# Attention and two feed-forward layers: the second layer's first product by Strassen's seven half-size products

## The chip, the cores and the metric

The kernel runs on one core of a Trainium2 chip. The metric is device time in microseconds (us) of one execution; of three runs of the kernel before, the median was 1325.76 us (1323.91 to 1326.36).

## The reference

Attention with four sink keys and a window of 128 over 4 batches of 8 heads, 768 positions, head size 64, gives x of 3072 tokens by 512. Two feed-forward layers follow, each with weights of its own (512 by 2048 and 2048 by 512):

```
x = softmax(keep(q @ k.T / 8)) @ v          # 3072 x 512, float32
h = x @ w1_in;  x = (h - tanh(h)) @ w1_out  # layer 1
h = maximum(x @ w2_in, 0);  out = (h * h) @ w2_out   # layer 2
```

All is float32.

## The kernel before

**Arithmetic.** A float32 operand is split into a high part (rounded to the format that TensorE multiplies in one pass) and a low part, the rest; `split` (L138) makes the high part on ScalarE and the low part on VectorE or GpSimd. A product is then three matmuls: high by high, high by low, low by high. The weights come as pairs of 32-bit words; `convert` (L124) makes float32 of them, with one ScalarE instruction and three VectorE instructions (L130 to L132) on integers, and splits the result.

**Tiling.** Both layers work on tiles of T = 384 tokens, NT = 8 of them. The hidden size 2048 is FC = 16 chunks of 128. For each tile j and chunk fc, `mm1` (L441) computes the chunk of h in one PSUM bank: 4 pieces of the 512 inputs, three matmuls each, the weights stationary and 384 tokens moving. `act` (L445) applies the nonlinearity (L452 and L453 in layer 1, L455 and L456 in layer 2) and splits it into gs. `mm2` adds the chunk to the output's accumulators in PSUM, in layer 1 with 12 matmuls of 384 tokens (L473), in layer 2 with 9 of 512 columns (L475). `mm2` of a chunk comes one chunk behind `mm1`, or two (`lag`) in the last tile of layer 1 and in layer 2, where `mm1` takes four PSUM banks in turn. Behind a tile's last chunk, ScalarE and VectorE copy the accumulators to two buffers o (L484, L482), and a DMA writes them to c.x2 in DRAM (L486) or to the output (L488).

**Stages.** Attention of tile 0 comes first. Then, during tile j of layer 1, attention of tile j + 1 runs between the matmuls (`Heads.tick`: score L257 to L261, its reduction on VectorE L262, exponential L269, normalization L279, transposes L309 and L322, product with v L346 to L364). In tile 0, `hook` also converts layer 1's weights. `hook` loads layer 2's weights from the last tile of layer 1 on, into the slots that layer 1's weights leave, and converts one chunk (of both matrices) every 1.4 chunks, through that tile and the first of layer 2. There `fetch` also loads and splits x of layer 2.

**Order.** TensorE runs in the order in which the program is written. The other engines and the DMA queue on SP get theirs from a planner, by priority and its own estimate of when things are ready; on the chip each engine then takes its instructions strictly in that order. `issue_after` keeps a block's instructions behind a named one on its engine.

Of the kernel before, what the change touches and what calls it, by code (L numbers as in the profile page):

```python
# [11 lines left out]
F32 = mybir.dt.float32  # L12
# [7 lines left out]
P = 128  # L20
# [13 lines left out]

FULL = 2 * H
OFF = 11
LEAD = 3
TMP = 8

# [81 lines left out]
    return c.wp.tile([P, 2, DM], dtype, tag=f"{tag}{i}", name=f"{tag}{i}", bufs=1)  # L121


def convert(c, raw, dst):  # L124

    nc = c.nc
    lo, hi = raw[:, :, 0], raw[:, :, 1]
    w = c.sb.tile([P, DM], I32, tag="w_bit", name="w_bit", bufs=3)
    nc.scalar.activation(hi.bitcast(F32), hi.bitcast(F32), AF.Copy, scale=2.0 ** -112)
    nc.vector.tensor_scalar(w, hi, 3, None, ALU.logical_shift_left)  # L130
    nc.vector.scalar_tensor_tensor(w, lo, 29, w, ALU.logical_shift_right, ALU.bitwise_or)  # L131
    nc.vector.scalar_tensor_tensor(w, hi, -2147483648, w, ALU.bitwise_and, ALU.bitwise_or)  # L132
    dst = dst()
    split(c, dst, w.bitcast(F32), nc.gpsimd)
    return dst


def split(c, dst, src, lo_eng):  # L138

    nc = c.nc  # L140
    nc.scalar.activation(dst[:, 0, :], src, AF.Copy)  # L141
    lo_eng.tensor_tensor(dst[:, 1, :], src, dst[:, 0, :].bitcast(F32), ALU.subtract)  # L142
# [22 lines left out]
class Heads:  # L165
# [200 lines left out]
    def gather(self, n):  # L366

        c, nc, s = self.c, self.c.nc, self.st[n]
        h = self.coords(n)[3]
        if h % 2 == 0:  # L370
            self.xf = c.sb.tile([P, T], F32, tag="xf", name="xf", bufs=2)
        dst = self.xf[D * (h % 2) : D * (h % 2) + D, :]
        if n < FULL:
            nc.scalar.activation(dst, s.av[:D, :T], AF.Copy)
            return
        t = c.sb.tile([D, T], F32, tag="t_av", name="t_av", bufs=2)
        nc.scalar.activation(t, s.av[D:, :T], AF.Copy)
        nc.vector.tensor_tensor(dst, s.av[:D, :T], t, ALU.add)

# [44 lines left out]

def ffn(c, layers, xs, hook=None):

    nc = c.nc
    accs = {}

# [15 lines left out]
    def act(l, h, j, fc):  # L445
        t = c.fp.tile([P, T], F32, tag="t", name="t", bufs=2)
        if lag(l, j) > 1 and fc % 2:
            gs = c.sb.tile([P, 3 * WN], F32R, tag="p", name="p", bufs=2)[:, : 2 * T].rearrange("p (a t) -> p a t", t=T)
        else:
            gs = c.fp.tile([P, 2, T], F32R, tag="gs", name="gs", bufs=2)  # L450
        if l == 0:
            c.last_a = nc.scalar.activation(t, h[:, :T], AF.Tanh)  # L452
            c.last_d = nc.vector.tensor_tensor(t, h[:, :T], t, ALU.subtract)  # L453
        else:
            c.last_a = nc.scalar.activation(t, h[:, :T], AF.Relu)  # L455
            c.last_d = nc.vector.scalar_tensor_tensor(t, h[:, :T], 0.0, t, ALU.max, ALU.mult)  # L456
        split(c, gs, t, nc.vector if l > 0 or j > 0 else nc.gpsimd)
        return gs

    def mm2(l, j, fc, gs, q):  # L460
        w = layers[l].get(1, fc)
        if fc == 0 and q == 0:
            accs[l, j] = [c.ps.tile([P, 512], F32, tag="acc", name="acc", bufs=4) for _ in range(KC if l == 0 else T // P)]
        acc = accs[l, j]
        pas = ((0, 0), (0, 1), (1, 0))
        n = len(acc)
        work = [(m, i) for m in range(n) for i in range(3)]
        hw = (len(work) + 1) // 2
        for m, i in work[q * hw : (q + 1) * hw]:
            a, b = pas[i]  # L470
            st = dict(start=(fc == 0 and i == 0), stop=(fc == FC - 1 and i == 2))
            if l == 0:
                nc.tensor.matmul(acc[m][:, :T], w[:, a, ts(m, P)], gs[:, b, :], **st)  # L473
            else:
                nc.tensor.matmul(acc[m], gs[:, b, ts(m, P)], w[:, a, :], **st)  # L475
        if fc == FC - 1 and q == 1:
            for m in range(n):
                o = c.fp.tile([P, 512], F32, tag="o", name="o", bufs=2)
                wd = T if l == 0 else 512
                with c.tc.high_priority(offset=200):  # L480
                    if m % 2:
                        nc.vector.tensor_copy(o[:, :wd], acc[m][:, :wd])  # L482
                    else:
                        nc.scalar.activation(o[:, :wd], acc[m][:, :wd], AF.Copy)  # L484
                if l == 0:
                    nc.sync.dma_start(c.x2[j, m], o[:, :T])  # L486
                else:
                    nc.sync.dma_start(c.out[j * T + m * P : j * T + (m + 1) * P, :], o)  # L488

    pend = []  # L490
    for l in range(2):
# [22 lines left out]
    for p in pend:  # L514
        mm2(*p, 0)
        mm2(*p, 1)


def fetch(c, src):

    x = []
    for kc in range(KC):
        f = c.sb.tile([P, T], F32, tag="xf", name="xf", bufs=2)
        c.nc.sync.dma_start(f, src(kc))
        t = c.xp.tile([P, 2, T], F32R, tag="x", name="x", bufs=8)
# [12 lines left out]


def banded(c):  # L540

    nc, tc = c.nc, c.tc
    with ExitStack() as es:
        pools(c, es)
        layers = [Weights(c, c.w1_in, c.w1_out), Weights(c, c.w2_in, c.w2_out)]
        heads = Heads(c, None)
        x2 = {}
        loaded = 0

        def next_chunk():  # L550
# [23 lines left out]
        done = 0  # L574

        def hook(l, j, fc, q):
            nonlocal done
            if l == 0:
                if j == 0 and q % 2 == 0:
                    next_chunk()  # L580
                f = fc + LEAD - (q == 1)
                if j == 0 and q % 2 == 1 and LEAD <= f < FC:
                    with tc.issue_after(c.last_a.ins), tc.issue_after(c.last_d.ins):
                        layers[0].convert(int(q == 1), f)
                if j + 1 < NT:
                    heads.tick(64 * (j + 1) + OFF + 4 * fc + q)
            tt = (l * NT + j - NT + 1) * FC + fc
            if q == 2 and 2 <= tt < FC + 2:
                for i in range(2):
                    layers[1].load(i, tt - 2)  # L590
            if q == 3:
                while done < FC and 5 + 1.4 * done <= tt:
                    with tc.issue_after(c.last_a.ins), tc.issue_after(c.last_d.ins):
                        for i in range(2):
                            layers[1].convert(i, done)
                    done += 1
            jn = l * NT + j + 1
            if jn >= NT and jn < 2 * NT and fc == 8 and q == 3:
                x2[jn - NT] = fetch(c, lambda kc: c.x2[jn - NT, kc])

        xs = lambda l, j: heads.x[j] if l == 0 else x2[j]
        with tc.manual_schedule(engines={mybir.EngineType.PE}):
            ffn(c, layers, xs, hook)


def general(c):
# [50 lines left out]
    with ExitStack() as es:  # L657
# [3 lines left out]
        def xs(l, j):  # L661
# [8 lines left out]
            return fetch(c, lambda kc: c.x2[j, kc])  # L670

        ffn(c, layers, xs)


@with_exitstack
def kernel(ctx: ExitStack, tc: tile.TileContext, a0, a1, vs, scal,
# [57 lines left out]
```

## Time and profile before

| what | us |
|---|---|
| median of three runs | 1325.76 |
| profiled execution | 1324.8 |
| its span, first to last instruction | 1323.0 |
| TensorE busy | 1271.1 |
| VectorE busy | 692.7 |
| ScalarE busy | 641.1 |
| GpSimd busy | 322.5 |

PE is TensorE's matmuls, PEld its weight loads, DVE VectorE, ACT ScalarE, POOL GpSimd, SP the engine that issues the DMAs. Matmuls overlap each other, so a matmul's own duration is longer than the time from its start to the next one's start. "Idle before" is the time in which an engine had nothing to do before an instruction, and what ended it.

### The profile page before, as it was taken

What the parts mean: (1) busy time and instruction counts of PE and PEld (TensorE: products, weight loads), DVE (VectorE), ACT (ScalarE), POOL (GpSimd) and SP (SyncE); (2) the same over time, 40 slices, a digit from 0 to 9 for tenths busy, and PEclk for the clock granted to TensorE, in tenths of its full rate; (3) what the DMA queues carried; (4) which work ended last, traced back from release to release, by engine and by line L of the source; (5) the groups of instructions that cost most, each with busy time, mean ns of one, the idle gap of its engine ahead of it and who ended that gap; (6) DMA issues with size and microseconds to landing.
All of it is one profiled execution on the core that took longest, in us unless ns stands there. A gap on an engine that the chain in (4) does not pass through costs nothing.

```text
span 1323.0 us, 19096 instructions
## 1 busy us (share of the span) xinstructions
PE 1271.1 (96%) x7152; PEld 1195.9 (90%) x7152; DVE 692.7 (52%) x1568; ACT 641.1 (48%) x1588; POOL 322.5 (24%) x299
## 2 busy tenths in 40 slices
PE   8888899999999999999998988999999999999997
PEld 5777799999999999999998977899999999999996
DVE  7788655666656665556654999322222222222222
ACT  7765665666656666666653555323232323232221
POOL 1555633333323333333321454201010101010000
PEclk9999999999999999999999999999999999999999
DMA  9641221211211212112007830101010101010000
GB/s 366 230 172 43 80 71 58 80 56 48 72 54 58 81 48 69 54 57 81 20 21 233 247 116 1 48 1 48 0 48 1 49 1 48 1 37 1 25 0 27
DMA packets 31814, 91.01 MB, mean 69 GB/s; under 512 B 3664, under 2 KB 11856, under 8 KB 31712
## 3 DMA queue, kind: packets, MB, share of 16 engines
q1 hardware_dynamic: 31712, 89.70, 20.4%
q8 instruction: 58, 0.95, 0.3%
q14 instruction: 44, 0.36, 0.1%
HBM read 77.11 MB, written 12.58 MB: 68 GB/s over the span
## 4 chain that ended last, share of the span: by engine, by line
PE 44%; DVE 3%; issue 3%; DMA 1%; ACT 1%; POOL 0%; SPq 0%; ACTq 0%; DVEq 0%; POOLq 0%
PE acc L475 19%; PE ps_h L441 6%; PE ps_v L441 5%; PE ps_s L441 5%; PE ps_t L441 5%; PE acc L473 2%; DVE w_bit L132 1%; DMA x<-o 1%; DVE w_bit L131 1%; DVE w_bit L130 0%; DMA xf<-x 0%; DVE t L453 0%; DVE p L142 0%; ACT o L484 0%; POOL x L142 0%
## 5 line engine op out<-in xcount | busy, mean ns | idle before, releaser
L441 PE MATMUL ps_h<-x,wi 128*128 128x384 f32 x1776 | 364.3, 343 | 0.8 <-DVE t L453 0.8
L441 PEld LDWEIGHTS ps_h<-x,wi 128*128 128x128 f32 x1776 | 305.8, 189 | 4.8 <-DVE t L453 1.8
L473 PE MATMUL acc<-gs,wo 128*128 128x384 f32 x1440 | 298.9, 344 | 10.4 <-ACT o L484 9.3
L473 PEld LDWEIGHTS acc<-gs,wo 128*128 128x128 f32 x1440 | 246.9, 189 | 14.9 <-ACT o L484 11.1
L142 POOL TENSOR_TENSOR x<-xf,x 128x384 fp32r<-128x384 f32 x64 | 66.8, 1051 | 411.9 <-ACT x L141 409.4
L475 PE MATMUL acc<-wo,gs 128*128 128x512 f32 x576 | 146.2, 397 | 4.2 <-DVE gs L142 2.0
L475 PE MATMUL acc<-wo,p 128*128 128x512 f32 x576 | 143.4, 393 | 1.1 <-DVE p L142 0.9
L141 ACT ACTIVATE gs<-t 128x384 fp32r<-128x384 f32 x184 | 96.3, 524 | 78.0 <-DVE t L456 38.1
L475 PEld LDWEIGHTS acc<-wo,gs 128*128 128x128 f32 x576 | 107.7, 189 | 25.9 <-DVE gs L142 2.7
L209 POOL TENSOR_TENSOR k_l<-qkv,k_h 128x416 fp32r<-128x416 f32 (+1 forms) x48 | 59.5, 1241 | 291.2 <-ACT k_h L208 291.1
L475 PEld LDWEIGHTS acc<-wo,p 128*128 128x128 f32 x576 | 107.1, 188 | 20.9 <-DVE p L142 1.4
L142 DVE TENSOR_TENSOR gs<-t,gs 128x384 fp32r<-128x384 f32 x168 | 97.3, 579 | 41.8 <-ACT gs L141 41.8
L262 DVE CUSTOM_DVE_ANT_0 p<-ps_s,m 128x272 f32<-128x272 f32 (+1 forms) x168 | 70.0, 416 | 87.7 <-PE ps_s L261 86.3
L453 DVE TENSOR_TENSOR t<-ps_h,t 128x384 f32<-128x384 f32 x116 | 64.6, 557 | 88.4 <-ACT t L452 88.4
L269 ACT ACTIVATE p<-p,nm 128x272 f32<-128x272 f32 (+1 forms) x168 | 83.3, 496 | 1.1 <-DVE nm L262 1.1
L441 PE MATMUL ps_v<-x,wi 128*128 128x384 f32 x432 | 82.4, 339 | 0.0
L441 PE MATMUL ps_t<-x,wi 128*128 128x384 f32 x432 | 82.2, 338 | 0.0
L441 PE MATMUL ps_s<-x,wi 128*128 128x384 f32 x432 | 81.7, 337 | 0.0
L441 PEld LDWEIGHTS ps_v<-x,wi 128*128 128x128 f32 x432 | 77.7, 190 | 2.8
L441 PEld LDWEIGHTS ps_t<-x,wi 128*128 128x128 f32 x432 | 77.5, 190 | 2.7
L279 DVE TENSOR_SCALAR p<-p,sm 128x272 f32<-128x272 f32 (+1 forms) x168 | 78.4, 490 | 2.3
L441 PEld LDWEIGHTS ps_s<-x,wi 128*128 128x128 f32 x432 | 77.0, 189 | 2.8
(130 smaller groups left out, 1771.9 us busy)
## 6 DMA issues: line engine op xcount, KB each, us to landing
qkv<-in_a_dram SPq DMA_DIRECT2D x32, 608.0 KB, 3.9
wi<-in_w_in_dram SPq DMA_DIRECT2D x32, 512.0 KB, 4.9
wo<-in_w_out_dram SPq DMA_DIRECT2D x32, 512.0 KB, 4.7
qkv<-in_a_dram SPq DMA_DIRECT2D x24, 504.0 KB, 3.5
x<-o SPq DMA_DIRECT2D x32, 192.0 KB, 3.4
xf<-x SPq DMA_DIRECT2D x32, 192.0 KB, 2.4
out_dram<-o SPq DMA_DIRECT2D x24, 256.0 KB, 2.0
wi<-in_a_dram SPq DMA_DIRECT2D x8, 504.0 KB, 7.5
```

The lines of the kernel that those rows point to most:

```text
L131: nc.vector.scalar_tensor_tensor(w, lo, 29, w, ALU.logical_shift_right, ALU.bitwise_or)
L132: nc.vector.scalar_tensor_tensor(w, hi, -2147483648, w, ALU.bitwise_and, ALU.bitwise_or)
L141: nc.scalar.activation(dst[:, 0, :], src, AF.Copy)
L142: lo_eng.tensor_tensor(dst[:, 1, :], src, dst[:, 0, :].bitcast(F32), ALU.subtract)
L209: nc.gpsimd.tensor_tensor(s.kl[:, :nk], s.k[:, :nk], s.kh[:, :nk].bitcast(F32), ALU.subtract)
L262: nc.vector.tensor_tensor_reduce(out=s.p[:, u, :w], in0=sc[:, :w], in1=self.masks[kind], op0=ALU.add, op1=ALU.min, scale=-SCALE / 2 if ful ...
L269: self.mark[n] = nc.scalar.activation(s.p[:, u, :w], s.p[:, u, :w], AF.Exp, bias=s.nm[:, u : u + 1], scale=-1.0, accum_out=s.sm[:, u : u + 1])
L279: nc.vector.tensor_scalar(s.p[:, u, :w], s.p[:, u, :w], s.sm[:, u : u + 1], None, ALU.mult)
L441: nc.tensor.matmul(h[:, :T], w[:, a, kc, :], x[kc][:, b, :], start=(kc == 0 and i == 0), stop=(kc == KC - 1 and i == 2))
L453: c.last_d = nc.vector.tensor_tensor(t, h[:, :T], t, ALU.subtract)
L473: nc.tensor.matmul(acc[m][:, :T], w[:, a, ts(m, P)], gs[:, b, :], **st)
L475: nc.tensor.matmul(acc[m], gs[:, b, ts(m, P)], w[:, a, :], **st)
```

## The change

The 2048 hidden columns of layer 2 are paired into NG = 8 groups of two chunks, the 512 inputs into two halves, and the tokens into tiles of 512, of two halves of 256. The first product of a group is then a 2 by 2 block product, done with seven block products (Strassen's scheme in Winograd's form) in place of eight. Each is two input pieces by three matmuls of 256 tokens. `first` does four of them, each in its own bank, `rest` three, which are added to banks in use; between and behind them stand the two halves of the second product of the group before. The sums of products are formed by VectorE from PSUM. The sums of weight blocks are formed by `split_in` in the last tile of layer 1, as layer 1's slots come free, and then stay in SBUF; the sums of x by GpSimd (`sum_x`), once for each tile of 512. The scheme's operands are split into high and low parts behind the sums.

Layer 2's weights are converted during tiles 1 to 6 of layer 1 (`early_step`, once a chunk, in half chunks) and written to DRAM: w_in as float32 (c.wi2), w_out already split (c.wo2). `fetch_out` reads w_out for every group again, into four slots. The pool sb of attention is closed at the start of layer 1's last tile, and a pool l2 takes its place; two buffers in sb become one.

```diff
-def convert(c, raw, dst):
+def to_single(c, raw, w):
...
+def convert(c, raw, dst):
+    w = c.sb.tile([P, DM], I32, tag="w_bit", name="w_bit", bufs=3)[:, : raw.shape[1]]
+    to_single(c, raw, w)
     dst = dst()
-    split(c, dst, w.bitcast(F32), nc.gpsimd)
+    split(c, dst, w.bitcast(F32), c.nc.gpsimd)
...
-            self.xf = c.sb.tile([P, T], F32, tag="xf", name="xf", bufs=2)
+            self.xf = c.sb.tile([P, T], F32, tag="xf", name="xf", bufs=1)
...
+    def early_step(self, step):
+        c = self.c
+        with c.tc.issue_after(c.last_a.ins), c.tc.issue_after(c.last_d.ins):
+            if step < 2 * FC:
+                if step == 0:
+                    self.load(c.w2_in, 0)
+                self.convert_in(step)
+                if step + 1 < 2 * FC:
+                    self.load(c.w2_in, step + 1)
+            elif step % 2 == 0:
+                self.load(c.w2_out, step // 2 - FC)
+            else:
+                self.convert_out(step // 2 - FC)
+
+    def fetch_out(self, fc):
+        c, k = self.c, fc % 4
+        if k < 2:
+            t = slot(c, ("wi", "wo")[k], FC - 1, F32R)
+        else:
+            t = c.l2.tile([P, 2, DM], F32R, tag=f"wos{k}", name=f"wos{k}", bufs=1)
+        c.nc.sync.dma_start(t.bitcast(F32), c.wo2[fc])
+        self.wo[fc] = t
...
+    def split_in(self, g):
...
+        for out, x, y in ((t1[:, 0], b2[:, 0], b1[:, 0]), (t1[:, 1], b2[:, 1], t1[:, 0]),
+                          (t2[:, 0], b2[:, 1], b2[:, 0]), (t2[:, 1], b1[:, 1], t1[:, 1])):
+            nc.vector.tensor_tensor(out, x, y, ALU.subtract)
...
+            nc.scalar.activation(d[:, :, 0, :], src, AF.Copy)
+            nc.vector.tensor_tensor(d[:, :, 1, :], src, d[:, :, 0, :].bitcast(F32), ALU.subtract)
...
+    def before(self, fc):
+        for g in range(NG):
+            if fc == (NP * g + 6) // 4 + 2:
+                self.split_in(g)
+                if g + 2 < NG:
+                    self.load_in(g + 2)
+        if fc == FC - 1:
+            for f in range(2):
+                self.fetch_out(f)
...
+    def product(self, j, g, name, bank, start):
+        w, x = self.w[g, name], self.x[j, name]
+        for kc in range(2):
+            for i, (a, b) in enumerate(((0, 0), (0, 1), (1, 0))):
+                self.c.nc.tensor.matmul(bank, w[:, a, kc, :], x[:, b, kc, :], start=start and kc == 0 and i == 0,
+                                        stop=kc == 1 and i == 2, skip_group_check=True)
+
+    def first(self, j, g):
...
+        for name, bank in zip(ORDER, s.ps):
+            self.product(j, g, name, bank, True)
+        nc.scalar.activation(s.u[:, 0, :], s.ps[0], AF.Copy)
+        nc.vector.tensor_tensor(s.u[:, 1, :], s.ps[1], s.u[:, 0, :], ALU.add)
+        nc.vector.tensor_tensor(s.u[:, 2, :], s.ps[2], s.u[:, 1, :], ALU.add)
+        nc.vector.tensor_tensor(s.c[:, 0, :], s.ps[3], s.u[:, 2, :], ALU.add)
...
+    def rest(self, j, g, s):
+        nc = self.c.nc
+        for name, i in zip(ORDER[4:], (0, 2, 3)):
+            self.product(j, g, name, s.ps[i], False)
...
+    def second(self, j, g, s, q):
...
+        seen = ((1, 1), (0, 0)), ((1, 0), (0, 1))
+        for th, f in seen[q]:
+            w, gs = self.wo[2 * g + f], s.g[th, f]
+            for m in range(2):
+                for i, (a, b) in enumerate(((0, 0), (0, 1), (1, 0))):
+                    nc.tensor.matmul(self.acc[2 * th + m], gs[:, b, ts(m, P)], w[:, a, :],
+                                     start=(g == 0 and q == 0 and i == 0), stop=(g == NG - 1 and q == 1 and i == 2))
...
         def hook(l, j, fc, q):
...
+            if 1 <= j < NT - 1 and q == 3:
+                second.early_step((j - 1) * FC + fc)
+            if j == NT - 1:
+                if fc == 0 and q == 0:
+                    c.sb_es.close()
+                    second.open()
+                if q == 3:
                     with tc.issue_after(c.last_a.ins), tc.issue_after(c.last_d.ins):
+                        second.before(fc)
...
-            ffn(c, layers, xs, hook)
+            second.run(ffn(c, layers, lambda l, j: heads.x[j], hook))
```

`open` loads x of the first 512 tokens (1 MB) and w_in of two groups (1 MB), and sums and splits x. `run` goes through the 48 groups in the order first, half of the second product of the group before, rest, the other half; with the first group stand layer 1's last two `mm2`.

## Rows read from the trace of the kernel before

**Rows 1.** The page's first part: busy us, share, count of each engine.
```profile
PE 1271.1 (96%) x7152; PEld 1195.9 (90%) x7152; DVE 692.7 (52%) x1568; ACT 641.1 (48%) x1588; POOL 322.5 (24%) x299
```
**Rows 2.** Busy time by stretches: from:to and length, busy (instructions), clock, DMA.
```profile
95.00:170.30 75.30, 65.03 (x366) 59.70 (x365) 52.89 (x108) 48.64 (x124) 46.17 (x38) 0.98 0.19 62
...
255.70:345.60 89.90, 88.56 (x573) 88.16 (x572) 55.63 (x147) 56.68 (x153) 29.48 (x30) 1.00 0.19 59
...
696.60:777.00 80.40, 73.32 (x400) 72.05 (x399) 61.34 (x83) 36.29 (x72) 27.80 (x21) 0.96 0.69 215
777.00:849.60 72.60, 67.23 (x321) 58.33 (x320) 57.48 (x83) 35.07 (x70) 26.95 (x21) 0.98 0.12 39
849.60:1310.60 461.00, 461.00 (x2316) 418.19 (x2315) 127.43 (x228) 130.02 (x255) 20.06 (x20) 1.00 0.06 20
```
**Rows 3.** Order of time on ACT: start, us, instruction; layer 2's first and seventh tile ends.
```profile
850.18 0.60 ACT L484 ACTIVATE o<-acc 128x512 f32<-128x512 f32 x1
...
1251.62 0.60 ACT L484 ACTIVATE o<-acc 128x512 f32<-128x512 f32 x1
```
**Rows 4.** Order of time on PE in layer 2.
```profile
1261.15 2.27 PE L441 MATMUL ps_h<-x,wi 128*128 128x384 f32 x12
1263.26 2.24 PE L475 MATMUL acc<-wo,gs 128*128 128x512 f32 x9
1265.34 1.92 PE L441 MATMUL ps_s<-x,wi 128*128 128x384 f32 x10
```
**Rows 5.** Order of time on PE beside attention, matmuls of 256 columns.
```profile
311.50 0.28 PE L350 MATMUL ps_v<-pt,v_s 128*128 128x256 f32 x1
311.61 0.28 PE L353 MATMUL ps_v<-pt,v_s 128*128 128x256 f32 x1
311.73 0.22 PE L350 MATMUL ps_v<-pt,v_s 128*128 128x128 f32 x1
```
**Rows 6.** Groups by line on DVE: count, busy us, mean ns, idle before.
```profile
L131 DVE SCALAR_TENSOR_TENSOR w_bit<-wi,w_bit 128x512 int32<-128x512 int32 x32 | 32.7, 1023 | 0.4
...
L132 DVE SCALAR_TENSOR_TENSOR w_bit<-wi,w_bit 128x512 int32<-128x512 int32 x32 | 25.8, 805 | 0.0
...
L130 DVE TENSOR_SCALAR w_bit<-wi 128x512 int32<-128x512 int32 x32 | 14.6, 457 | 1.6 <-issue 0.7 <-ACT wi L129 0.4
...
L296 DVE TENSOR_TENSOR pt<-ps_t,pt 128x256 fp32r<-128x256 f32 x24 | 10.0, 417 | 0.3 <-ACT pt L294 0.3
```
**Rows 7.** DMA issues: count, KB each, median us from issue to landing.
```profile
wo<-in_w_out_dram SPq DMA_DIRECT2D x32, 512.0 KB, 4.7
```
**Rows 8.** Order of time on DVE and PE in tile 0.
```profile
101.41 0.69 DVE L131 SCALAR_TENSOR_TENSOR w_bit<-wo,w_bit 128x512 int32<-128x512 int32 x1
102.14 1.63 DVE L132 SCALAR_TENSOR_TENSOR w_bit<-wo,w_bit 128x512 int32<-128x512 int32 x1
...
104.19 1.27 PE L257 MATMUL ps_s<-qkv 128*128 128x272 f32 x2 [2.80 <-DVE nm L262]
```
**Rows 9.** Waits: who waited for whom, us in total, times, longest.
```profile
PE acc L473 <- ACT o L484: 9.3, 7, 3.4
```
**Rows 10.** Order of time at the start of layer 1's last tile.
```profile
703.52 0.49 ACT L484 ACTIVATE o<-acc 128x384 f32<-128x384 f32 x1 [5.03 <-DMA x<-o]
...
704.07 2.02 PE L473 MATMUL acc<-gs,wo 128*128 128x384 f32 x6 [3.38 <-ACT o L484]
...
705.89 3.13 PE L441 MATMUL ps_v<-x,wi 128*128 128x384 f32 x12
...
708.86 2.24 PE L473 MATMUL acc<-p,wo 128*128 128x384 f32 x12
```
**Rows 11.** Order of time near the end of layer 1's last tile.
```profile
771.71 3.10 PE L473 MATMUL acc<-p,wo 128*128 128x384 f32 x11 [2.31 <-DVE p L142]
```
**Rows 12.** Order of time at the turn to layer 2, evictions.
```profile
777.00 0.48 ACT L484 ACTIVATE o<-acc 128x384 f32<-128x384 f32 x1
...
780.82 0.49 ACT L484 ACTIVATE o<-acc 128x384 f32<-128x384 f32 x1 [1.68 <-DMA x<-o]
```

More of the change, by code (lines that the diff above doesn't have):

```diff
@@ L36 @@
 OFF = 11
+T2 = 512
+HT = T2 // 2
+NG = FC // 2
+NP = 7
 LEAD = 3
@@ L375, in gather @@
             return
-        t = c.sb.tile([D, T], F32, tag="t_av", name="t_av", bufs=2)
+        t = c.sb.tile([D, T], F32, tag="t_av", name="t_av", bufs=1)
         nc.scalar.activation(t, s.av[D:, :T], AF.Copy)
@@ L447, in act @@
         if lag(l, j) > 1 and fc % 2:
-            gs = c.sb.tile([P, 3 * WN], F32R, tag="p", name="p", bufs=2)[:, : 2 * T].rearrange("p (a t) -> p a t", t=T)
+            gs = c.spare(fc)[:, : 2 * T].rearrange("p (a t) -> p a t", t=T)
         else:
@@ L485, in mm2 @@
                 if l == 0:
-                    nc.sync.dma_start(c.x2[j, m], o[:, :T])
+                    nc.sync.dma_start(c.x2[m, :, ts(j, T)], o[:, :T])
                 else:
@@ L490, in ffn @@
     pend = []
-    for l in range(2):
+    for l in range(len(layers)):
         for j in range(NT):
@@ L513, in ffn @@
                 pend.append((l, j, fc, gs))
-    for p in pend:
-        mm2(*p, 0)
-        mm2(*p, 1)
+    return [lambda p=p, q=q: mm2(*p, q) for p in pend for q in range(2)]
 def fetch(c, src):
@@ L522, in fetch @@
     for kc in range(KC):
-        f = c.sb.tile([P, T], F32, tag="xf", name="xf", bufs=2)
+        f = c.sb.tile([P, T], F32, tag="xf", name="xf", bufs=1)
         c.nc.sync.dma_start(f, src(kc))
@@ L544, in banded @@
         pools(c, es)
-        layers = [Weights(c, c.w1_in, c.w1_out), Weights(c, c.w2_in, c.w2_out)]
+        layers = [Weights(c, c.w1_in, c.w1_out)]
         heads = Heads(c, None)
-        x2 = {}
+        second = Second(c)
         loaded = 0
@@ L573, in banded @@
                     layers[0].convert(i, fc)
-        done = 0
         def hook(l, j, fc, q):
[L577 to L582, printed above, removed]
-                    with tc.issue_after(c.last_a.ins), tc.issue_after(c.last_d.ins):
[L584 to L601, printed above, removed]
+            if j == 0 and q % 2 == 0:
+                next_chunk()
+            f = fc + LEAD - (q == 1)
+            if j == 0 and q % 2 == 1 and LEAD <= f < FC:
+                with tc.issue_after(c.last_a.ins), tc.issue_after(c.last_d.ins):
+                    layers[0].convert(int(q == 1), f)
+            if j + 1 < NT:
+                heads.tick(64 * (j + 1) + OFF + 4 * fc + q)
+            if 1 <= j < NT - 1 and q == 3:
[5 more added lines that the diff above has]
+                if q == 3:
+                    with tc.issue_after(c.last_a.ins), tc.issue_after(c.last_d.ins):
+                        second.before(fc)
         with tc.manual_schedule(engines={mybir.EngineType.PE}):
-            ffn(c, layers, xs, hook)
+            second.run(ffn(c, layers, lambda l, j: heads.x[j], hook))
 def general(c):
@@ L669, in xs @@
                 return fetch(c, lambda kc: c.x1[b * H + 2 * kc : b * H + 2 * kc + 2, :, half * T : (half + 1) * T].rearrange("h d s -> (h d) s"))
-            return fetch(c, lambda kc: c.x2[j, kc])
-        ffn(c, layers, xs)
+            return fetch(c, lambda kc: c.x2[kc, :, ts(j, T)])
+        for m in ffn(c, layers, xs):
+            m()
 @with_exitstack
@@ L684 @@
     c.x1 = dram.tile([B * H, D, S], F32, tag="x1", name="x1")
-    c.x2 = dram.tile([NT, KC, P, T], F32, tag="x2", name="x2")
+    c.x2 = dram.tile([KC, P, B * S], F32, tag="x2", name="x2")
+    c.wi2 = dram.tile([FC, P, DM], F32, tag="wi2", name="wi2")
+    c.wo2 = dram.tile([FC, P, 2, DM], F32, tag="wo2", name="wo2")
     scalars(c)
```

143 lines of the change are left out of this document (141 added, 2 removed).

## The prediction

> **What bounds the kernel now.** I read the first part of the page, then busy time by stretches cut at the tiles of 384 tokens, then TensorE's order of time. In the page [rows 1] the reader is to see that TensorE is busy for 96% and nobody else for more than 52%. The stretches [rows 2] say where the other 4% lies. From 255.7 to 345.6 us (one tile of layer 1 beside attention) TensorE is busy for 88.56 of 89.90 us; from 849.6 to 1310.6 us (layer 2 behind its first tile) for all of 461.00. So there the number of matmuls and the time of one decide. Between lie 696.6 to 849.6, the last tile of layer 1 and the first of layer 2, where time is lost while layer 2's weights are converted. A tile of layer 2 undisturbed takes (1251.62 - 850.18) / 6 = 66.91 us [rows 3]; the first one took 72.6, so 5.7 is lost. A tile of layer 1 without attention is 16 times 24 matmuls of 384 columns; 12 of these take 2.11 us from start to start [rows 4], so 67.5 us. The last one took 80.4: 12.9 lost. Together 18.6.
>
> **The first product (removed and added).** Now, each pair of weight chunks and 384 tokens takes 24 matmuls of 384 columns, 4.22 us; 8 tiles by 8 pairs make 64 x 4.22 = 270.1 us. Changed, each pair and 512 tokens takes seven products of six matmuls of 256 columns: 42, and 6 x 8 x 42 = 2016. A 256-column matmul appears with attention: two of them start at 311.50 and end their turn at 311.73 [rows 5], 0.115 us each. By the slope of the long ones (2.11 / 12 = 0.176 at 384 columns, 2.08 / 9 = 0.231 at 512) [rows 4] it would be 0.121. I take 0.118, between them, because the rows with 256 columns are only two in a row and rounded: 2016 x 0.118 = 237.9 us. **Saving 32.2 us**, with bounds of 26.2 (0.121) and 38.3 (0.115). The second product keeps 1152 matmuls of 512 columns, hence its time.
>
> The rest of the new layer must hide behind 42 x 0.118 + 24 x 0.231 = 10.5 us of TensorE for each group. VectorE has ten instructions in it, nine of 256 elements and one of 512: at 0.417 us for a 256-element one from PSUM [rows 6] and twice that for the long one, 4.6 us. ScalarE has six short ones. GpSimd has one subtraction a group and eleven longer ones a tile of 512; at its mean of 322.5 / 299 = 1.08 us [rows 1], (48 + 66) x 1.08 = 123 us in 504. In order of time: between the last of a group's seven products and its reuse of a bank stand at least 12 matmuls of 512 columns (2.77 us), and the squares are wanted a whole group later. TensorE fills in with the second product of the group before. So cost nothing; were this cover gone (a PSUM sum on the path, 0.417 us, in each of 48 groups) it would be 20 us. Reloading w_out: 1 MB a group, each of its two DMAs 4.7 us to landing [rows 7], asked for a group ahead: hidden by 10.5 us.
>
> **The weights' conversion (moved).** From the last tile of layer 1 and the first of layer 2 it goes into tiles 1 to 6 of layer 1, as 64 half chunks. A whole chunk takes VectorE 0.457 + 1.023 + 0.805 = 2.29 us [rows 6], a half about 1.2 with its fixed part. 64 x 1.2 = 77 us more VectorE. These tiles now have it busy for 55.63 of 89.90 us (62%) [rows 2]; tiles 1 and 2 get 16 halves each and rise to some 83%, tiles 3 to 6 get 8 each (some 72%). Average room is not the question: VectorE and the other queues are in order, and behind a conversion stand the score's reduction (L262), which frees the score's PSUM bank, the subtraction after tanh (L453), which frees the only bank of the first product, and attention's low parts. That is what tile 0 shows: L132 of a conversion from 102.14, then TensorE's score matmul at 104.19, 2.80 us late [rows 8]. The price of it there: 65.03 of 75.30 us busy [rows 2], 10.3 us lost with 26 whole chunks, or 0.2 us for a half. By this 64 halves cost 12.8 us. A gain is excluded, since TensorE has under 1.4 us idle in such a tile, at its end. I take half, **6 us**: a half chunk is three short instructions where tile 0 has two chunks in a row beside GpSimd's subtractions, and attention there runs in full precision mode. The steps' own DMAs (a load of 256 KB, a store of 128 or 256 KB) stand in SP's queue, each behind the conversion it waits for, ahead of q, k, v loads two heads early (cover: a head's 10 us) and of layer 1's stores. The latter matter: at tile ends TensorE waits for the output buffers already, 9.3 us in 7 times [rows 9]. I add **1 us**, bounds 0 and 6 (1 us in each of six ends).
>
> In the same rows L132 lasts 1.63 us and its mean is 0.805, so GpSimd beside it shows. The Trainium skill (SBUF — State Buffer, on the port pair that VectorE and GpSimd share) says that the one that starts first holds the pair for its whole instruction and the other fully blocks. The trace agrees with the long L132. Without it, an L131 takes 0.69 us [rows 8] where its mean is 1.023; if both logical instructions took that, a half would be 0.92 us and the 77 us would be 59, and the term of 6 would shrink towards 4.6.
>
> **The last tile of layer 1 and the turn.** Today's loss of 18.6 us goes, and three things are late next.
> (a) At its start the stores of the tile before compete with loads. Now ScalarE's eviction waits 5.03 us for its buffer, TensorE 3.38 us, and the 18 matmuls behind it run at about half speed (704.07 to 708.86 is 4.79 us, where 18 x 0.176 = 3.17) [rows 10]: 5.0 us. The change puts 2 MB of x and weights in the same place, where now 512 KB chunks come; I keep **5**, bounds 0 and 10.
> (b) Eight times, two chunks are combined (four VectorE subtractions of 256, then three of 512 and one of 256): about 5 x 0.417 + 3 x 0.83 = 4.6 us, 37 us in the tile, with 16 x 1.1 for its own: 55 of 67.5 us. Now the conversion's VectorE fills 61.34 of 80.40 [rows 2] and costs 12.9 - 5.0 = 7.9; TensorE waits 2.31 us at 771.71 for a low part [rows 11]. Less work without GpSimd beside it: I take **1**, bounds 0 and 7.9.
> (c) At the turn, the second product's first group needs the last accumulators and w_out's slot 15. The third eviction now starts 3.82 us after the first (777.00 to 780.82) [rows 12] for want of a buffer; the load of the slot starts only behind the last matmul of layer 1 and lasts 4.7 us [rows 7], while TensorE has 24 x 0.118 = 2.8 us of new products to do. That is 2 us late, and 1 for what the three stores beside it take: **3**, bounds 0 and 7.
> So 18.6 turns into 9: **9.6 us gained**, bounds 18.6 and, with all three at their worst, 6 lost.
>
> **Others.** Five ends of 512-token tiles have four evictions instead of three with two buffers: 1 us in all, bounds 0 and 5; the tail's fourth eviction 0.3.
>
> **Sum.** -32.2 - 9.6 + 6 + 1 + 1.3 = -33.5 us. The profiled execution took 1324.8 us (span 1323.0 and 1.8 around it): 1291.3. The median of the runs is 1.0 above it: 1292.3, put at 1292.
>
> **The rivals.**
> R1, all clean: the combining, the turn and the conversions hide wholly and (a) goes. For it: tiles 1 to 6 lose only at their ends today. Against: 2 MB of loads in (a). 1292 - 6 - 9 = 1277.
> R2, losses stay: the last tile and the turn cost today's 18.6, the conversions tile 0's price of 12.8. 1292 + 9.6 + 6.8 = 1308. For it [rows 8]; against, less VectorE work in both places.
> R3, slower: the conversions become the bound of tiles 1 to 6, at VectorE's queue ahead of the score's reduction. Tile 0's wait of 2.80 us comes with two whole chunks, four halves: 0.7 us a half, 64 x 0.7 = 45 us instead of 6: 1331. It decides from 0.6 us a half on (39.5 / 64). Against: of 26 chunks in tile 0 a few alone paid that.
> R4, slower: weight loads bind. Every matmul loads 128 columns, and the changed layer has 3168 of them instead of 2688. In layer 2 loads are busy for 418.19 us in 2315 [rows 2], 0.181 each; 3168 x 0.181 = 573 us instead of 504: 1292 + 69 = 1361. Against: two matmuls with a load each within 0.23 us [rows 5], so loads overlap. The Trainium skill (Perfetto Trace Analysis, Identifying the Most-Contended Engine) takes the busy share of LDWEIGHTS for TensorE's roofline, not that of matmuls; by that rule layer 2 at 91% has no room for 18% more loads, and R4 would hold. The trace bears it out little.
>
> **Chances.** Forecast 0.62 (1284 to 1301), R1 0.14, R2 0.14, R3 0.07, R4 0.03. Faster by over 0.2% (about what a measurement of this kernel tells from none): forecast, R1, R2, less the edge of R2: 0.88. Within 0.2%: 0.03, from between R2 and R3. Slower: 0.09. The range reaches from R1 to a little beyond R2: 1277 to 1312.
>
> **What would show it.** The product line has 2016 matmuls of 256 columns, starting 0.118 us apart; TensorE 100% busy in layer 2, with 63 us for six groups. Tiles 1 to 6 are 1 us longer on average, with waits for L262, L453 or L279. TensorE's waits for evictions stay at the last tile's start, and one of about 3 us stands at the turn. Wrong would be: matmuls 0.125 us or more apart, tiles 1 to 6 longer by over 3 us each, or TensorE under 97% in layer 2.

## The result and the profile after

The changed kernel takes 1303.9 us (median of 4, 1303.17 to 1305.74) against 1326.06 us beside it: 0.9837 of the time, 95% interval 0.982 to 0.9855. Forecast was 1292, the range 1277 to 1312. The profiled execution took 1303.22 us, its span 1301.3, 21.7 us less than before.

The page's first part, after [rows 1]:

```profile
PE 1245.7 (96%) x7632; PEld 1167.3 (90%) x7632; DVE 816.4 (63%) x2004; ACT 644.6 (50%) x1690; POOL 396.5 (30%) x381
```

TensorE is still busy for 96%. VectorE has 124 us more. Where this lies is told by the stretches, cut where a tile's first accumulator is evicted (from:to and length, busy us of PE, PEld, DVE, ACT, POOL with instructions, clock, DMA) [rows 2]:

```profile
170.80:260.80 90.00, 88.51 (x547) 84.93 (x546) 68.13 (x197) 59.78 (x166) 28.66 (x30) 1.00 0.44 131
260.80:360.70 99.90, 91.76 (x567) 86.99 (x567) 74.55 (x193) 62.35 (x167) 29.96 (x29) 1.00 0.39 117
...
716.40:787.00 70.60, 67.71 (x404) 67.39 (x403) 51.22 (x103) 36.91 (x76) 16.96 (x13) 1.00 0.32 100
787.00:875.00 88.00, 85.51 (x529) 77.35 (x528) 45.16 (x93) 22.90 (x58) 25.40 (x23) 0.98 0.37 117
875.00:1291.50 416.50, 416.13 (x2599) 376.27 (x2598) 206.81 (x442) 111.17 (x274) 83.68 (x79) 1.00 0.38 119
```

The second of these is tile 2 of layer 1: 99.9 us where it was 89.9. The last is layer 2 behind its first tile, with TensorE busy all the time. Layer 2's order of time on PE (start, us, instruction) [rows 4]:

```profile
1001.14 2.91 PE L747 MATMUL acc<-wos,x 128*128 128x512 f32 x12
1003.89 0.88 PE L696 MATMUL ps_h<-xop,wi 128*128 128x256 f32 x6
1004.60 0.88 PE L696 MATMUL ps_s<-xop,wo 128*128 128x256 f32 x6
1005.32 0.88 PE L696 MATMUL ps_t<-xop,wi 128*128 128x256 f32 x6
1006.04 0.88 PE L696 MATMUL ps_v<-xop,wo 128*128 128x256 f32 x6
1006.76 1.55 PE L747 MATMUL acc<-wo,x 128*128 128x512 f32 x6
```

Four products take 2.87 us, so a matmul of 256 columns starts every 0.120 us; the second product's 12 take 2.75.

Put together by stretches, in us of the spans:

| stretch | before | after | difference | forecast |
|---|---|---|---|---|
| up to tile 0's end | 169.8 | 170.8 | +1.0 | 0 |
| tiles 1 and 2 | 175.8 | 189.9 | +14.1 | } +7 |
| tiles 3 to 6 | 351.0 | 355.7 | +4.6 | } |
| last tile of layer 1, 67.5 clean | 80.4 | 70.6 | -9.8 | } -9.6 |
| first tile of layer 2, above a clean one | 6.3 | 3.8 | -2.5 | } |
| layer 2's tiles, clean (8 x 66.91, 6 x 84.16) | 535.3 | 505.0 | -30.3 | -32.2 |
| other ends of layer 2 | 4.5 | 5.5 | +1.1 | +1.3 |

(A tile is measured from its predecessor's first eviction to its own, hence 6.3 where the prediction's stretch gave 5.7.) The differences were taken before rounding and sum to -21.7. One term is far off: the conversions in tiles 1 to 6 cost 18.7 us, not 7.

What TensorE and ScalarE wait for in tile 2 (who waited for whom: us, times, longest):

```profile
ACT wos L132 <- DMA wos<-in_w_in_dram: 15.9, 16, 2.3
ACT p L278 <- DVE nm L271: 12.9, 11, 2.0
...
PEld ps_s L269 <- DVE nm L271: 7.6, 7, 2.2
```

The first row is new: in each of the tile's 16 chunks ScalarE stands until the raw weights have landed. One such place in order of time:

```profile
295.87 0.37 SPq L574 DMA_DIRECT2D wos<-in_w_in_dram  x1
...
298.66 0.45 ACT L132 ACTIVATE wos<-wos 128x256 f32<-128x256 f32 x1 [0.96 <-DMA wos<-in_w_in_dram]
...
299.01 0.51 ACT L150 ACTIVATE gs<-t 128x384 fp32r<-128x384 f32 x1
...
299.54 0.49 ACT L386 ACTIVATE t_av<-ps_v 64x384 f32<-64x384 f32 x1
...
300.72 0.30 DVE L133 TENSOR_SCALAR w_bit<-wos 128x256 int32<-128x256 int32 x1
...
301.66 1.11 DVE L135 SCALAR_TENSOR_TENSOR w_bit<-wos,w_bit 128x256 int32<-128x256 int32 x1
302.69 0.43 DVE L271 CUSTOM_DVE_ANT_0 p<-ps_s,m 128x272 f32<-128x272 f32 x1
...
303.18 0.39 PE L269 MATMUL ps_s<-k_h,q_s 128*128 128x272 f32 x1 [1.30 <-DVE nm L271]
303.21 0.38 SPq L574 DMA_DIRECT2D wos<-in_w_in_dram  x1
```

The load is issued at 295.87 and used at 298.66, and meanwhile tanh's high part (L150) and attention's eviction (L386) stand behind it on ScalarE. VectorE's conversion then comes late, into the time of the score's reduction (L271), for which TensorE waits 1.30 us; L135 itself lasts 1.11 us here, where its mean is 0.456. The next load is issued only behind the conversion's last reader, since there is one buffer.

The conversion itself is as sized (DVE groups in tiles 1 to 6: count, busy, mean ns, idle before): 1.18 us for a half chunk, forecast 1.2.

```profile
L135 DVE SCALAR_TENSOR_TENSOR w_bit<-wos,w_bit 128x256 int32<-128x256 int32 x64 | 29.2, 456 | 2.0
L134 DVE SCALAR_TENSOR_TENSOR w_bit<-wos,w_bit 128x256 int32<-128x256 int32 x64 | 27.8, 435 | 0.7
...
L133 DVE TENSOR_SCALAR w_bit<-wos 128x256 int32<-128x256 int32 x64 | 18.5, 288 | 12.4 <-ACT wos L132 12.2
```

The turn to layer 2 [rows 12], in order of time:

```profile
789.74 0.38 SPq L609 DMA_DIRECT2D wo<-wo  x1
...
789.81 0.48 ACT L494 ACTIVATE o<-acc 128x384 f32<-128x384 f32 x1
...
791.95 0.54 DVE L492 COPY o<-acc 128x384 f32<-128x384 f32 x1
```

And TensorE's own order of time behind it:

```profile
793.87 2.62 PE L747 MATMUL acc<-wo,x 128*128 128x512 f32 x6 [2.49 <-DMA wo<-wo]
796.29 2.15 PE L747 MATMUL acc<-wi,x 128*128 128x512 f32 x6
798.28 0.88 PE L696 MATMUL ps_h<-xop,wi 128*128 128x256 f32 x6
```

The load of w_out's second chunk, issued at 789.74 behind layer 1's last matmul, is what TensorE waits for, 2.49 us. The wait costs more than its length: behind it the granted clock is 0.53 from 794 to 797 us, close to the lower of TensorE's two levels (1.2 of 2.4 GHz), and 1.00 again from 799 on. The 12 matmuls of 512 columns take 4.41 us where 12 others take 2.75, another 1.66.

### The profile page after: what moved, and what is told of

The parts are those of the page before. It is cut to its first block, busy times and chain, and to the rows that moved or that the text cites. A ratio compares the mean times of both kernels' runs of the same rounds, so it can differ in the third digit from the quotient of the medians.

```text
span 1301.3 us, 21253 instructions
## 1 busy us (share of the span) xinstructions
PE 1245.7 (96%) x7632; PEld 1167.3 (90%) x7632; DVE 816.4 (63%) x2004; ACT 644.6 (50%) x1690; POOL 396.5 (30%) x381
## 4 chain that ended last, share of the span: by engine, by line
PE 72%; DVE 10%; DMA 8%; ACT 4%; issue 2%; POOL 1%; SPq 0%; ACTq 0%; DVEq 0%; POOLq 0%
PE acc L747 20%; PE acc L483 14%; PE ps_h L451 12%; PE ps_h L696 5%; PE ps_v L696 5%; PE ps_t L696 5%; DMA wos<-in_w_in_dram 5%; DVE w_bit L135 3%; PE ps_s L696 3%; DMA x<-o 2%; DVE w_bit L134 2%; PE ps_t L318 2%; DVE w_bit L133 2%; PE ps_s L269 1%; PE ps_v L359 1%
## 5 line engine op out<-in xcount | busy, mean ns | idle before, releaser
L483 PE MATMUL acc<-gs,wo 128*128 128x384 f32 x1440 | 300.4, 346 | 10.3 <-ACT o L494 10.3
L451 PE MATMUL ps_h<-x,wi 128*128 128x384 f32 x1392 | 293.1, 346 | 1.0 <-DVE t L463 1.0
L451 PEld LDWEIGHTS ps_h<-x,wi 128*128 128x128 f32 x1392 | 238.1, 189 | 3.8 <-DVE t L463 3.0
L150 ACT ACTIVATE x<-gs 128x256 fp32r<-128x256 f32 x144 | 54.8, 412 | 203.9 <-DVE gs L713 130.1
L151 POOL TENSOR_TENSOR x<-gs,x 128x256 fp32r<-128x256 f32 x48 | 35.6, 741 | 351.0 <-ACT x L150 351.0
L747 PE MATMUL acc<-wos,x 128*128 128x512 f32 x576 | 139.5, 391 | 0.0
L747 PEld LDWEIGHTS acc<-wos,x 128*128 128x128 f32 x576 | 105.2, 188 | 19.9
L271 DVE CUSTOM_DVE_ANT_0 p<-ps_s,m 128x272 f32<-128x272 f32 (+1 forms) x168 | 69.6, 414 | 31.7 <-PE ps_s L270 29.9
L150 ACT ACTIVATE gs<-t 128x384 fp32r<-128x384 f32 x120 | 62.7, 523 | 30.1 <-DVE t L463 27.8
L747 PE MATMUL acc<-wo,x 128*128 128x512 f32 x288 | 74.8, 395 | 2.5 <-DMA wo<-wo 2.5
L747 PE MATMUL acc<-wi,x 128*128 128x512 f32 x288 | 74.9, 394 | 0.4 <-DVE o L754 0.4
L151 POOL TENSOR_TENSOR xop<-xs,xop 128x512 fp32r<-128x512 f32 x42 | 57.2, 1388 | 35.7 <-ACT xop L150 35.7
L303 ACT ACTIVATE pt<-ps_t 128x384 fp32r<-128x384 f32 (+1 forms) x112 | 51.6, 461 | 29.2 <-PE ps_t L318 28.4
L747 PEld LDWEIGHTS acc<-wo,x 128*128 128x128 f32 x288 | 53.1, 190 | 12.7 <-issue 2.7
L747 PEld LDWEIGHTS acc<-wi,x 128*128 128x128 f32 x288 | 53.0, 190 | 11.2 <-DVE o L754 1.1
```

What stands on the lines that cost most here:

```text
L271: nc.vector.tensor_tensor_reduce(out=s.p[:, u, :w], in0=sc[:, :w], in1=self.masks[kind], op0=ALU.add, op1=ALU.min, scale=-SCALE / 2 if ful ...
L303: nc.scalar.activation(hi, src, AF.Copy)
L451: nc.tensor.matmul(h[:, :T], w[:, a, kc, :], x[kc][:, b, :], start=(kc == 0 and i == 0), stop=(kc == KC - 1 and i == 2))
L747: nc.tensor.matmul(self.acc[2 * th + m], gs[:, b, ts(m, P)], w[:, a, :], start=(g == 0 and q == 0 and i == 0), stop=(g == NG - 1 and q == ...
```

## The experiments

Tiles are read from eviction to eviction; the last column is the time of one execution, or the median where several were timed. The planner's order of the engines shifts with each edit, so a few us in a stretch that an edit does not touch mean nothing: tiles 3 to 6 have the same program in the changed kernel, one_load, no_bits and narrow, and take 355.7 to 360.1 us.

| run | tiles 1, 2 | tiles 3 to 6 | last of layer 1 | first of layer 2 | time |
|---|---|---|---|---|---|
| before | 175.8 | 351.0 | 80.4 | (384 tokens) | 1326.06 |
| changed | 189.9 | 355.7 | 70.6 | 88.0 | 1303.9 |
| one_load | 177.8 | 360.1 | 72.4 | 86.2 | 1294.7 |
| no_bits | 175.5 | 359.6 | 70.5 | 87.7 | 1293.0 |
| prefetch | 180.0 | 362.5 | 73.4 | 88.0 | 1302.2 |
| stores_only | 175.5 | 351.6 | 71.9 | 86.6 | 1284.5 |
| both | 181.1 | 366.1 | 71.8 | 89.4 | 1306.4 |
| turn | 181.6 | 365.7 | 71.8 | 83.7 | 1301.1 |
| best | 181.2 | 365.3 | 72.1 | 83.7 | 1300.4 |
| swap | 188.8 | 369.1 | 76.4 | 86.4 | 1317.5 |
| ahead | 180.2 | 360.6 | 72.6 | 83.7 | 1294.1 |
| odd | 188.8 | 357.9 | 70.9 | 83.7 | 1300.2 |
| narrow | 189.8 | 358.4 | 71.6 | 84.1 | 1293.7 |

**Is it the conversions at all?** stores_only:

```diff
-                self.convert_in(step)
-                if step + 1 < 2 * FC:
-                    self.load(c.w2_in, step + 1)
...
+                c.nc.sync.dma_start(c.wi2[fc, :, ts(h, DM // 2)], self.kept.bitcast(F32))
```

> The changed kernel with one half chunk of each matrix converted, and the same tiles stored for all others (layer 2's weights are wrong): no loads, no ScalarE, VectorE, GpSimd work of 62 of 64 conversions; buffers and pools as in the changed kernel. Theories A and B: tiles 1 to 6 take about 528 us (526.8 before, 545.6 after), total about 1286. Theory C: most of the 18.8 us stays, total about 1300.

Measured: 527.2 us for tiles 1 to 6 (526.9 before), 1284.5 in all. The buffers that were cut from two to one, and the stores, cost nothing; the 18.7 us are the conversions' loads and engine work.

**ScalarE's wait for the load, or VectorE's instructions?** one_load:

```diff
                 self.convert_in(step)
-                if step + 1 < 2 * FC:
-                    self.load(c.w2_in, step + 1)
```

> The changed kernel, but w_in's first half chunk is loaded once and converted 32 times (layer 2's w_in is wrong); all conversion instructions stay, no ScalarE instruction waits for a load. Tiles 1 and 2 of layer 1 (first eviction to first eviction) took 175.8 us before and 189.9 after, +14.1. Theory A (ScalarE, in order, stands waiting for the raw weights' load, and attention behind it): 176 to 180 us, total about 1292. Theory B (the VectorE instructions that are added stand ahead of attention's): 187 to 190, total about 1302. Theory C (one buffer for xf and t_av where there were two): 190, total 1303.

Its evictions at the end of tiles 0 and 2:

```profile
170.29 0.47 ACT L494 ACTIVATE o<-acc 128x384 f32<-128x384 f32 x1
...
348.04 0.47 ACT L494 ACTIVATE o<-acc 128x384 f32<-128x384 f32 x1
```

Measured: 177.8 us, so without a wait for a load, and with all of the conversion's instructions, 12.1 of the 14.1 us are gone. (The other loads are gone too; prefetch, below, keeps them.) no_bits takes the three VectorE instructions away:

```diff
-        to_single(c, self.early, w)
+        c.nc.scalar.activation(w.bitcast(F32), self.early[:, :, 1].bitcast(F32), AF.Copy, scale=2.0 ** -112)
```

> The changed kernel without the three VectorE instructions of w_in's conversions (w_in of layer 2 is wrong): ScalarE writes the stored tile itself; load, ScalarE instruction and store stay, each load still asked for behind the conversion before. Theory A: the load is asked for some 2 us earlier, so the wait shrinks too: 177 to 183 us for tiles 1 and 2. Theory B: 176 to 178. Theory C: 190. Read with one_load: A says that this one is no faster than one_load, B that it is faster by 10 us or more.

Measured: 175.5 us, 2.3 less than one_load, neither A's "no faster" nor B's 10. But ScalarE still waits for loads here, and nothing is lost by it. In tiles 1 and 2 of the changed kernel and of no_bits:

```profile
ACT wos L132 <- DMA wos<-in_w_in_dram: 26.4, 30, 2.3
...
ACT w_bit L580 <- DMA wos<-in_w_in_dram: 11.2, 11, 2.2
```

So the two causes do not add up. VectorE's instructions without the wait cost 2.0 us (one_load against before), a wait of 11.2 us without them costs none, and the two together cost 14.1. The wait is needed for the loss, as one_load shows, and so is something that no_bits takes away: VectorE's instructions, or the rest of the wait. No run tells these two apart.

**The remedy, and where it falls short.** prefetch loads w_in into w_bit's three buffers:

```diff
-                if step == 0:
-                    self.load(c.w2_in, 0)
+                if step + 1 < 2 * FC:
+                    self.load_raw(step + 1)
                 self.convert_in(step)
-                if step + 1 < 2 * FC:
-                    self.load(c.w2_in, step + 1)
```

> The changed kernel, complete, with w_in's raw half chunks loaded one step ahead into w_bit's three buffers, so a conversion finds its load landed. Theory A: tiles 1 and 2 take 177 to 182 us, total 1292 to 1297. Theory B: 187 to 190, total 1301 to 1304. Theory C: no change.

Measured: tiles 1 and 2 as A had it, 180.0, so with all loads kept 9.9 of the 14.1 us are gone; in all 1302.2 (0.9813 of before, 0.9781 to 0.9845), not told from the changed kernel. Most of what tiles 1 and 2 gave, tile 3 took: 93.4 us instead of 86.2, and there ScalarE now waits for w_out's load (0.2 us in the changed kernel's tile 3), which still has one buffer for load, result and store; that this wait is what costs the 7 us is not shown:

```profile
ACT wos L132 <- DMA wos<-in_w_out_dram: 10.1, 5, 2.9
```

both loads everything ahead and spreads the conversions evenly:

```diff
+            if step % 3 == 2:
+                return
+            k = 2 * (step // 3) + step % 3
+            if k + 1 < 4 * FC:
+                self.load(k + 1)
+            (self.convert_in, self.convert_out)[k % 2](k // 2, self.raw.pop(k))
```

> The changed kernel, complete; the raw half chunks of both matrices go through w_bit's three buffers, each loaded one conversion ahead, and the 64 conversions are spread evenly (two of every three chunks, w_in and w_out in turn). Theory A (ScalarE in order waits for the raw load): no ScalarE wait for a raw load of over 0.5 us stays, tiles 1 to 6 take 529 to 535 us (545.6 in the changed kernel, 542.6 with the loads of w_in alone ahead), total 1288 to 1294. Theory B (VectorE's added instructions): spread, they cost as much in all, 540 to 546, total about 1300. Theory D (GpSimd and the stores of w_out in tiles 3 to 6): 536 to 540.

Measured: 547.2 us for tiles 1 to 6, total 1306.4 (0.9855, 0.9838 to 0.9871): no better than the changed kernel. ScalarE's waits for raw loads are all but gone in these tiles (3.3 us in 4 times):

```profile
ACT w_bit L132 <- DMA w_bit<-in_w_in_dram: 3.1, 3, 1.9
ACT w_bit L132 <- DMA w_bit<-in_w_out_dram: 0.2, 1, 0.2
```

So theory A alone falls. Something else costs as much: in tiles 3 to 6 the changed kernel's 32 conversions, all at odd chunks, cost 4.6 us, and these 43, at odd and even ones, 15.1.

**The place in attention's head.** A head takes two chunks, so odd and even are different halves of it. swap does w_out's conversions at the even ones:

```diff
-            elif step % 2 == 0:
-                self.load(c.w2_out, step // 2 - FC)
-            else:
-                self.convert_out(step // 2 - FC)
+            elif step > 2 * FC:
+                i = (step - 2 * FC - 1) // 2
+                if step % 2:
+                    self.load(c.w2_out, i)
+                if step % 2 == 0 or step == 6 * FC - 1:
+                    self.convert_out(i)
```

> The changed kernel, complete, with w_out's 32 half chunks converted at the even chunks of tiles 3 to 6 and loaded at the odd ones (the last one is loaded and converted in one place). A head of attention takes two chunks, so the work is the same and meets the other half of a head. Theory E (what a conversion costs hangs on which attention instructions of VectorE, ScalarE and GpSimd are queued behind it): tiles 3 to 6 take 365 us or more (355.7 in the changed kernel, 351.1 before), as the evenly spread run suggests, whose 43 conversions there, at both halves of a head, cost 15 us. Theory B' (so much VectorE time costs so much, wherever it stands): 354 to 358.

Measured: 369.1 us, 18.0 above before instead of 4.6, for the same work: 0.56 us a conversion against 0.14, or against 0.28 by the slowest of the other runs with the changed kernel's tiles 3 to 6 (360.1 us). (The last half chunk is loaded and converted in one place at tile 6's end; ScalarE waits 5.49 us there and TensorE not at all. The last tile, 76.4, is not read.) What happens, in order of time:

```profile
486.29 1.16 POOL L151 TENSOR_TENSOR x<-xf,x 128x384 fp32r<-128x384 f32 x1 [1.84 <-ACT x L150]
486.62 1.11 DVE L135 SCALAR_TENSOR_TENSOR w_bit<-wos,w_bit 128x256 int32<-128x256 int32 x1
...
487.82 0.42 ACT L150 ACTIVATE wos<-w_bit 128x256 fp32r<-128x256 f32 x1 [1.61 <-DVE w_bit L135]
...
488.27 0.49 ACT L303 ACTIVATE pt<-ps_t 128x384 fp32r<-128x384 f32 x1
...
488.79 0.56 DVE L305 TENSOR_TENSOR pt<-ps_t,pt 128x384 fp32r<-128x384 f32 x1 [0.70 <-ACT pt L303]
...
489.41 0.55 PE L318 MATMUL ps_t<-ident,p 128*128 128x128 f32 x3 [0.74 <-DVE pt L305]
```

L135 lasts 1.11 us beside GpSimd's subtraction of x; its mean is 0.593 in these tiles and 0.425 in the same tiles of the changed kernel. ScalarE stands 1.61 us for it, to make the weights' high part, and attention's transposes, behind it in the queue, are evicted late (L303, L305); TensorE waits 0.74 us for their bank. In tiles 3 to 6 there are 11 such waits (the changed kernel has one, of 1.5 us):

```profile
PE ps_t L318 <- DVE pt L305: 7.9, 11, 0.9
```

So here, too, ScalarE's order passes a delay on, with another producer in front. How long ScalarE stands for L135 is not the price by itself: that is 44.9 us in 29 times here and 33.6 in 32 in the changed kernel's tiles. What is queued behind it differs.

**The turn and the last tile.** turn is both with two slots exchanged:

```diff
-            t = slot(c, ("wi", "wo")[k], FC - 1, F32R)
+            t = slot(c, ("wi", "wo")[k], FC - 1 - k, F32R)
...
-        s.u = slot(c, ("wi", "wo")[g % 2], FC - 2, F32)
+        s.u = slot(c, ("wi", "wo")[g % 2], FC - 2 + g % 2, F32)
```

> As the run both, and w_out's second chunk goes into the slot wo14 (free behind the matmuls of chunk 14) and the sums u of odd groups into wo15, so the load is asked for some 4 us earlier. If that load alone makes TensorE wait at the turn (2.49 us in the changed kernel), the first tile of layer 2 takes 85.5 us instead of 88.0; if the accumulators' third and fourth eviction is late as well, 86 to 87.5.

Measured: 83.7 us, a clean tile, 4.3 less than changed and better than expected: the wait of 2.49 us and the 1.66 us of lower clock behind it went together (granted clock 1.00 in the whole tile). The load was the only wait; the third eviction comes before the matmul that needs its bank, which waits for nothing:

```profile
792.86 0.48 ACT L494 ACTIVATE o<-acc 128x384 f32<-128x384 f32 x1
...
794.02 1.55 PE L747 MATMUL acc<-wo,x 128*128 128x512 f32 x6
```

best also spreads the loads at the start of layer 1's last tile:

```diff
-        self.load_x(0)
         self.load_in(0)
-        self.load_in(1)
-        self.sum_x(0)
...
+                if fc == 2 and q == 0:
+                    second.load_in(1)
+                if fc == 4 and q == 0:
+                    second.open_x()
```

> As the run turn, and at the start of layer 1's last tile only 512 KB of w_in are loaded; 512 KB more at chunk 2 and 1 MB of x at chunk 4. If the loads (2 MB) make the stores of the tile before late, TensorE's wait of 2.89 us there falls to 1 us and the last tile takes 68.5 us instead of 70.6; if a store takes that long by itself, 70.6 stays. Total by theory A 1285 to 1290.

Measured: 72.1 us for the last tile, against 71.8 in turn: nothing gained, total 1300.4 (0.9815, 0.9798 to 0.9831). At the tile's start TensorE waits 2.5 us in turn, and not for an eviction or a store but for ScalarE's high part of gs; in best it no longer waits there, but 2.87 us later on, at 741 us, for VectorE's low part. Either wait has a stretch of lower clock behind it: 11 matmuls take 3.58 us in turn and 3.52 in best, at a granted clock of 0.52 and 0.53, where 1.9 us is usual.

**Together.** ahead is turn with the conversions back in their places:

```diff
+            if step >= 2 * FC and step % 2 == 0:
+                return
+            k = step if step < 2 * FC else 2 * FC + (step - 2 * FC) // 2
```

> As the run turn, but the conversions stand where the changed kernel has them (w_in at each chunk of tiles 1 and 2, w_out at the odd chunks of tiles 3 to 6), all raw chunks loaded one conversion ahead. Theories A and E together: 180 us in tiles 1 and 2 (as prefetch), 352 to 356 in tiles 3 to 6, total 1284 to 1289. Theory B': 545 in all six, total about 1299.

Measured: 180.2 us as expected, 360.6 in tiles 3 to 6 instead of 352 to 356 (355.7 to 360.1 in the runs that leave them alone), total 1294.1 (0.9757 of before, 0.9738 to 0.9777): the fastest complete version, below the changed kernel's interval. odd puts w_in's conversions at odd chunks, two in a row:

```diff
+            ks = [step - 1, step] if step < 2 * FC else [2 * FC + (step - 2 * FC) // 2]
```

> As the run ahead, but w_in's conversions go to the odd chunks of tiles 1 and 2 alone, two in a row. Theory E: tiles 1 and 2 take 177 to 179 us (180.0 with one at each chunk and the loads ahead, 175.8 before); if two in a row block for longer than attention has room, 182 or more.

Measured: 188.8 us, the time of the second case. VectorE's subtraction after tanh, which frees the first product's bank, is late, and TensorE waits for it 5.4 us in 9 times, as it would if two in a row are longer than the room that attention leaves. But they also want more of w_bit's buffers at once (VectorE waits 10.3 us for their stores in these two tiles, ScalarE 8.6 for loads), so the run does not separate the two.

**What paces a matmul of 256 columns?** narrow:

```diff
+                n = HT if start and kc == 0 and i == 0 else 192
-                self.c.nc.tensor.matmul(bank, w[:, a, kc, :], x[:, b, kc, :],
+                self.c.nc.tensor.matmul(bank[:, :n], w[:, a, kc, :], x[:, b, kc, :n],
```

> The changed kernel with 192 instead of 256 columns in all matmuls of the seven products but the first of each of the four in first (a quarter of layer 2's sums is left out). In the changed kernel they start 0.120 us apart. If the moving columns set that, 192 columns start 0.088 to 0.092 us apart; if the load of 128 weight columns does, 0.107 to 0.120 stays.

```profile
1004.86 0.81 PE L697 MATMUL ps_h<-xop,wi 128*128 128x192 f32 x6
1005.51 0.83 PE L697 MATMUL ps_t<-xop,wi 128*128 128x192 f32 x6
1006.18 0.83 PE L697 MATMUL ps_v<-xop,wo 128*128 128x192 f32 x6
1006.85 1.58 PE L748 MATMUL acc<-wi,x 128*128 128x512 f32 x6
```

Six of 192 columns take 0.65 to 0.67 us, 0.108 to 0.112 each, not 0.09. By the slope the columns would allow 0.09; something with a floor near 0.11 takes over, and the weight load is the part of a matmul that the edit leaves as it was (that it is the load is argued; no run changed it). The Trainium skill (TensorE: Matmul & The Clock Gate, LDWEIGHTS) gives a load's time in ns as its columns over 1.2, by which 128 columns take an estimated 107 ns; the spacing of 0.108 to 0.112 us agrees, while the row of a single load lasts 0.19 us in the trace (at 299.02 in the changed kernel) and overlaps the next one's. At 256 columns the products stand 0.01 us above the pace of narrow. It is no least spacing for every case: three of attention's transposes of 128 columns start 0.08 us apart (299.27 to 299.51 in the changed kernel, with loads of 128 columns).

## Why the prediction was right, and where not

The total of 1303.9 lies in the range, but not between 1284 and 1301, where the forecast itself was put, and it is nearer to R2's 1308 than to 1292. The range holds it because it reached to R2, and of R2's two losses only one came: the conversions' (18.7 against its 12.8), while the last tile and the turn did not keep theirs. That it is inside is partly luck. And one of the prediction's own signs of being wrong came true: tiles 1 to 6 are longer by 18.7 / 6 = 3.1 us each, over the 3 that it named.

**The first product** (-32.2, measured -30.3) was right in mechanism. The matmul takes 0.120 us, at the upper bound (0.121 by slope) and not at my 0.118 from two rounded rows; this makes -28.2, and the second product's matmuls, at 0.229 instead of 0.231, give the other 2. All other work of layer 2 is hidden, as said: TensorE 416.13 of 416.50 us busy.

**The conversions** are the step that failed in size: "I take half, 6 us", and 1 for the stores' queue, against 18.7. The VectorE time was right (1.18 us a half chunk) and the price was not. The steps' loads I put behind the conversions in SP's queue and looked only for who else waits there; that the conversion itself waits for the load, with one buffer and a load of 2.9 us, and that its first instruction stands on ScalarE in front of tanh and exponential, was not in the sum. one_load shows that without this wait 12.1 us are gone, prefetch 9.9 with the loads kept; no_bits shows that a wait of 11.2 us costs nothing by itself. The rest is what the prediction named, attention's instructions queued behind a conversion, in the places shown on ScalarE as well as on VectorE; its price depends on the place (0.14 to 0.56 us), which one average over tile 0 cannot tell. R3 put the queue on VectorE alone, at 0.7 us; no run shows that price.

**The last tile and the turn** (-9.6, measured -12.3): (a) TensorE's wait at the start came as said, 2.89 us (3.38 before), without the slow stretch behind it (granted clock 1.00 from 722 to 726 us, where it was 0.64 from 704.07 to 708.86 before); (b) cost nothing; (c) 3.8 with the wait of 2.49 us for w_out's slot, forecast 3. That it came near has luck in it: the 2 us of the load were 2.49, and the rest is the lower clock behind the wait, not the stores. That the evictions are late too was wrong: turn removes it all with the load alone.

R1 fell with the conversions, R2 with the last tile. R4 fell by its share: with 3168 loads in layer 2 instead of 2688 PEld is busy for 376.27 of 416.50 us, 90.3%, where it was 90.7 [rows 2]. So a busy share counts overlapped loads and is no floor; narrow shows where the pace of these products stops falling, and where R4 took 0.181 for each load, a load and its matmul of 256 columns together take 0.120.

Left open: tiles 3 to 6 take 360.6 us in ahead and 355.7 in the changed kernel, with the conversions in the same places; the planner's order differs, and no run tells which difference costs the 5 us. The runs that leave these tiles as in the changed kernel take up to 360.1, so the 355.7 may be the lucky one, and the 4.6 us of the conversions there a low reading. Between one_load's 177.8 and ahead's 180.2 lie the loads themselves, or their order.

## What to carry to other kernels

Work that is moved beside other work brings its loads along: on an engine that runs in order, an instruction that waits for a DMA stops everything behind it, so give its input a second buffer and ask one step ahead before judging its compute time. Whether such a wait costs anything depends on what else is late: here it cost nothing where VectorE had no conversion to do. Where that other work has a period, the place in it can matter more than the amount (here two to four times), and spreading evenly can lose what a good place gives. A wait of TensorE can cost more than its length, by the lower clock behind it. Before cutting matmul columns, measure narrower ones with the same loads: below some width the time stops falling with the columns.

## What the runs showed of the hardware

Matmuls of 256 columns with a 128-column weight load each start 0.120 us apart for 24 in a row, and with 192 columns 0.108 to 0.112: somewhere between, the moving columns stop setting the pace. A VectorE instruction with two SBUF inputs that meets a GpSimd one lasted 1.11 us (L135 at 486.62) where its mean is 0.456. Behind a wait of TensorE of 2.49 us the granted clock fell to 0.53 from 794 to 797 us, and 12 matmuls of 512 columns took 4.41 us instead of 2.75; behind one of 2.89 us (723.94) it stayed at 1.00.
